# Two accumulating transfers become VectorE additions, and a list scheduler is given ranks

## The chip, the core and the metric

The kernel runs on one core of a Trainium2 chip. TensorE multiplies matrices (at most 128x128 weights against 128x512 data here) into eight banks of PSUM; VectorE, ScalarE and GpSimd work element by element; transfers are started from queues of SyncE (SP), ScalarE and GpSimd and run on 16 DMA engines that these queues share. The metric is the device time of one execution in microseconds.

## The reference

Three layers follow each other, in fp32, for a batch of 2 and a sequence of 768: retention attention with 8 heads of 64, a gated network (`moe`), and a gated network that mixes along the sequence (`moe2`). Cut to what matters:

```python
state = gamma * state + einsum('bhd,bhe->bhde', k[:, :, t], v[:, :, t])   # attention, over t
y[:, :, t] = scale * einsum('bhd,bhde->bhe', q[:, :, t], state)

xk = mu_k * x + (1 - mu_k) * x_prev                  # moe
k = np.maximum(xk @ w_k, 0.0)                        # w_k: 512 x 1024
v = k * k @ w_v                                      # w_v: 1024 x 512
x = v / (1 + exp(-(xr @ w_r)))

h = gelu(x @ w_in); u, v = halves of h               # moe2
v_s = einsum('ts,bsd->btd', w_sg, normalised v) + b_sg
out = x + (u * v_s) @ w_out
```

## The kernel before, in words

Every fp32 product is made of three products of halves: each operand is split into a high part (rounded) and a low part (the rest), and high x high, high x low and low x high are summed in PSUM. `dense` (L326) issues them as three groups. A split is a cast, on ScalarE or VectorE, whichever comes first, and a subtraction on VectorE.

The sequence is done in three blocks of 256 positions (both batches, so 512 columns). Block 0 takes `w_k` and `w_v` directly (`k_tile`, `v_tile`). Blocks 1 and 2 together are done by a Strassen-Winograd scheme with seven products instead of eight: `k_first`, `k_second`, `k_n6`, `k_n5`, `k_m3`, `k_n7`, `k_m4` for `w_k`, and the `v_` functions for `w_v`. The scheme needs sums of quarters of the weights. Those of `w_k` are built in two buffers of the pool `raw`, `k1` and `k3` (128 x 1024): `k_sum_new` starts one on VectorE, `k_sum_dve` (L631) adds one quarter's half on VectorE, and `k_sum_add` (L626) adds one by a transfer from GpSimd's queue that accumulates into `raw`. `k1` goes through three stages that build on each other: after the adds of `aB` half 1 it is split into `s1`, after those of `aA` half 0 into `s2`, and after those of `aA` half 1 into `s4`; `k3` is split into `s3`. The split (`k_split`, L636) writes over quarters of `w_k` that are no longer read. `aA` and `aB` are the two halves of the columns of `w_k`, each with a high and a low tile. In the same way the sums of `w_v` are built by `sum_weights` (L753): an SP transfer starts a sum and GpSimd transfers (L762) accumulate into it.

What sets the order of all this is the class `Plan`. The program is written down as a list of operations, each with an engine, a reckoned cost and its dependences. `order` plays them through: whenever an engine is free, it takes the first operation in the list that is ready and for which there is a buffer. "ADD" stands for GpSimd's queue of accumulating transfers; before, one was reckoned as landing like an ordinary transfer of its size. The order that results is fixed for each engine: an engine runs its instructions one after the other, and one that waits keeps back all behind it.

TensorE's stages, by the names of their outputs in PSUM: `kp` (products with `w_k`), `rp` (with `w_r`), `vp` (with `w_v`, and again with the `v` half of `w_in`), `up` (the `u` half), `sp` (mixing with `w_sg`), `op` (with `w_out`).

Of the kernel before, what the change touches and what calls it, by code (L numbers as in the profile page):

```python
# [47 lines left out]
SLACK = {"raw": 2.0}  # L48
BEGIN = 0.75
ISSUE = 0.4  # L50
ADD_ISSUE = 1.2
DMA_LEAD = 1.4
DMA_TAIL = 2.0
DMA_RATE = 0.41
# [6 lines left out]
class Plan:  # L61


    def __init__(self, slots, quota, most):
        self.ops, self.writer, self.readers, self.users, self.origin = [], {}, {}, {}, {}
        self.slots, self.quota, self.most = slots, quota, most

    def op(self, eng, cost, fn, r=(), w=(), new=(), after=()):
        n = len(self.ops)
        deps = set(after)  # L70
        for k in r:
            deps.update(self.writer.get(k, ()))
        for k in w:
            deps.update(self.writer.get(k, ()))
            deps.update(self.readers.get(k, ()))
        for k in (*r, *w):
            if k[0] in self.origin:
                deps.add(self.origin[k[0]])
        for _, _, buf, _ in new:
            self.origin[buf] = n  # L80
        for k in w:
            self.writer[k], self.readers[k] = [n], []
        for k in r:
            if k not in w:
                self.readers.setdefault(k, []).append(n)
        for k in (*r, *w):
            self.users.setdefault(k[0], set()).add(n)
        self.ops.append((eng, cost, fn, deps, new))

    def order(self):  # L90
        ops, n = self.ops, len(self.ops)
# [19 lines left out]
        link2 = 0.0  # L111
        started = [False] * n

        def put(i):
# [26 lines left out]
            return True  # L141

        def start(i, t, eng):
            nonlocal link, link2
            engs, cost, fn, deps, new = ops[i]
            engs = engs.split()
            if len(engs) > 1:
                cost = cost[engs.index(eng)]
            for e in engs:
                queue[e].remove(i)  # L150
            on[i] = eng
            started[i] = True
# [26 lines left out]
        while events:  # L179
            t = events[0][0]  # L180
            while events and events[0][0] <= t + 1e-9:
                _, i, eng = heapq.heappop(events)
                if eng in SLACK:
                    free[eng] += 1
                elif 0 <= i < n:
                    for k in after[i]:
                        if (ops[k][0] == on[i]) == (eng == "near"):
                            left[k] -= 1
                            if not left[k]:
                                put(k)  # L190
# [21 lines left out]
def fused_kernel(ctx, tc, qk, kv, w_k, w_v, w_r, w_in, w_sg, w_out, consts, ydec, b_sg, out):  # L212
# [11 lines left out]
    T = {}  # L224
# [43 lines left out]
    def convert(name, j, src, dst, tag, part, first):  # L268
# [34 lines left out]
        plan.op("DVE", .69, join, r=[(raw, 1)], w=[(xb, 0)])  # L303
# [430 lines left out]
    def both(out, one, two, op, new=(), sign=None):  # L734
        def go():
            if sign is None:
                dve.tensor_tensor(out=T[out], in0=T[one], in1=T[two], op=op)
            else:
                dve.scalar_tensor_tensor(out=T[out], in0=T[one], scalar=sign, in1=T[two], op0=ALU.mult, op1=op)
        plan.op("DVE", 1.23 if sign is None else 1.32, go, r=[(b, i) for b in (one, two) for i in range(2)], w=[(out, i) for i in range(2)], new=new)  # L740

    def combine(at, one, two, op, first=()):
        (buf, part, view), (ba, pa, va), (bb, pb, vb) = at, one, two
# [140 lines left out]
    for j in range(8):  # L884
        conv("wk", w_k, j, ("aA", "aB"))
    for j in range(8):
        k_tile(0, j)
# [4 lines left out]
    k_first(0)  # L892
    for j in range(1, MK):
        k_first(j)
        k_second(j - 1)
    k_second(MK - 1)
    for m in range(KD):
        prep(0, m, 1)
        conv("wr", w_r, m, ("cA",))
# [1 line left out]
        r_tile(0, m)  # L901
    for m in range(KD):
        for j in range(2):
            conv("wv", w_v, 2 * m + j, ("bA", "bB"))
# [3 lines left out]
    k_sum_dve("k3", "aA", 0, 1)  # L908
    k_sum_add("k1", "aB", 1, 0)
    k_sum_add("k1", "aB", 1, 1)  # L910
    for m in range(KD):
        prep(1, m, 1)
    for m in range(KD):
        r_tile(1, m)
    for m in range(KD):
        prep(2, m, 0, term(2, m), False)
    k_terms()
    for m in range(MK):
        pair_relu(("kf", 1, m // 2), m, 1.0)
# [9 lines left out]
    k_operands("t1", 1, 0)  # L929
    k_n5()  # L930
    for m in range(KD):
        prep(2, m, 1)
    k_split("k3", "s3", "aA", 0, "s2")
    k_split("k1", "s4", "aA", 1)
    k_operands("b22", 2, 1)
    for m in range(MK):
        k_m3(m)
    k_operands("t3", 2, 0)
    k_operands("t4", 1, 1)
    k_n7(0)  # L940
    k_n7(1)
    k_m4(0)
    k_m4(1)
    v_terms(0)
    k_n7(2)
    k_n7(3)
    k_m4(2)
    k_m4(3)
    v_terms(1)
    for m in range(KD):  # L950
        r_tile(2, m)
    v_sums()
    v_direct(1)
    v_weights()
    v_n6()
    v_n5()
    v_sums2()
    v_sums3()
    v_n7()
    for m in range(KD):  # L960
        prep2(0, m)
        conv("win", w_in, m, ("aB", "aA"))
    v_m3()
    v_m4()
    for m in range(KD):
        conv("win", w_in, KD + m, ("aB", "aA"))
        prep2(1, m)
    for m in range(KD):
        prep2(2, m)

# [252 lines left out]
            gating(1, 0, m, half(v), (v, 0), -1)  # L1223

    for j in range(4):
        conv("wout", w_out, j, ("cA",))
    for n in range(NB):
        for b in range(B):
            c1(n, b)
        for m in range(KD):  # L1230
            c2(n, m)
        if n == 0:
            sg("g11", [(0, 0)], "bA", 0)
            sg("g12", [(0, 1)], "bA", 1)
        if n == 1:
            sg("g2", [(0, 0), (1, 0), (1, 1)], "bB", 0)
# [4 lines left out]
    sg_sum("g3", [(0, 0), (1, 0)])  # L1241
    for n in range(NB):
        g_terms(n)
    g_second()
    g_n6()
    g_n5()
    sg_sum("g4", [(0, 0), (0, 1), (1, 0), (1, 1)])
    sg_split("g3", "bA", 0)
# [93 lines left out]
```

## Time and profile before

| | us |
|---|---|
| median of 3 runs | 364.12 (363.67 to 364.89) |
| the profiled execution | 365.24 |
| its span, first to last instruction | 363.5 |
| TensorE busy in the span | 342.7 |
| VectorE, ScalarE, GpSimd busy | 281.2, 194.5, 45.7 |

The profiled execution is 1.12 us above the median. A span is cut by the last instruction; 1.74 us of the execution lie outside it. "Busy" counts the time in which an engine has an instruction at work. A releaser is what ended the idle time of an engine by the profile; where the releaser had itself been waiting, one looks further up its own queue.

### The profile page before, as it was taken

The numbers are of one execution on the slowest core, as the hardware profiler recorded it, in microseconds if no ns is written. First come the engines' busy times: TensorE is split into PE (matmuls) and PEld (weight loads), VectorE is DVE, ScalarE is ACT, GpSimd is POOL, SyncE is SP. The second block draws the span as 40 slices with busy tenths as digits, with TensorE's granted clock in tenths as the row PEclk, the third lists the DMA queues.
The fourth block names the chain that finished last, engine by engine and source line by source line (L and its number), as shares of the span: only waits on it lengthen the run. The fifth ranks groups of instructions, "written<-read, shape, count | busy, mean of one in ns | idle before, by whom it ended". The sixth has DMA issues, their size and how long they took to land.

```text
span 363.5 us, 5464 instructions
## 1 busy us (share of the span) xinstructions
PE 342.7 (94%) x2121; PEld 292.8 (81%) x2121; DVE 281.2 (77%) x479; ACT 194.5 (54%) x306; POOL 45.7 (13%) x42
## 2 busy tenths in 40 slices
PE   8998999999999358699999999999999999999996
PEld 4886888888888246587887888888888999999995
DVE  2599999899976362758989999954658999999832
ACT  1068889799953160656979968822222563514000
POOL 0454400000133222141000000122110000000000
PEclk9999999999999959699999999999999999999999
DMA  8999951136277979396323533899840000000422
GB/s 303 411 409 405 367 175 61 60 115 231 94 119 118 169 152 160 125 176 105 86 89 115 175 115 115 262 207 224 199 65 0 2 2 0 2 0 2 172 88 87
DMA packets 23145, 52.36 MB, mean 144 GB/s; under 512 B 1744, under 2 KB 12368, under 8 KB 23120
## 3 DMA queue, kind: packets, MB, share of 16 engines
q1 hardware_dynamic: 14144, 38.45, 29.4%
q0 software_dynamic: 8688, 12.52, 21.4%
q10 hardware_dynamic: 288, 1.05, 0.7%
q8 instruction: 16, 0.26, 0.3%
q14 instruction: 9, 0.07, 0.1%
HBM read 38.38 MB, written 3.15 MB: 114 GB/s over the span
## 4 chain that ended last, share of the span: by engine, by line
PE 71%; DMA 18%; DVE 4%; issue 3%; ACT 1%; POOL 1%; SPq 0%; DVEq 0%; POOLq 0%; ACTq 0%
PE vp L334 19%; PE kp L334 15%; PE sp L334 11%; PE op L334 9%; PE up L334 9%; PE rp L334 6%; DMA chunk<-kv 6%; DMA raw<-wv 5%; DMA raw<-wk 4%; DMA chunk<-qk 2%; DMA raw<-raw 1%; DVE cv L297 1%; PE y L506 1%; DVE prs L442 1%; DVE raw L623 1%
## 5 line engine op out<-in xcount | busy, mean ns | idle before, releaser
L334 PE MATMUL kp<-xo,wk 128*128 128x512 f32 x264 | 63.8, 401 | 4.3 <-ACT ku L680 4.3
L334 PEld LDWEIGHTS kp<-xo,wk 128*128 128x128 f32 x264 | 50.7, 194 | 16.3 <-ACT ku L680 4.7
L334 PE MATMUL vp<-k,wv 128*128 128x512 f32 x168 | 41.2, 405 | 9.4 <-ACT k L256 9.4
L334 PEld LDWEIGHTS vp<-k,wv 128*128 128x128 f32 x168 | 33.1, 198 | 16.9 <-ACT k L256 9.8
L334 PE MATMUL sp<-sg,vh 128*128 128x384 f32 x252 | 44.6, 335 | 0.1
L334 PEld LDWEIGHTS sp<-sg,vh 128*128 128x128 f32 x252 | 43.7, 188 | 0.8 <-ACT vh L256 0.7
L334 PE MATMUL op<-gt,wout 128*128 128x384 f32 x192 | 33.6, 334 | 0.0
L334 PEld LDWEIGHTS op<-gt,wout 128*128 128x128 f32 x192 | 33.3, 188 | 0.0
L334 PE MATMUL rp<-xo,wr 128*128 128x512 f32 x144 | 33.3, 389 | 0.0
L334 PE MATMUL vp<-win,x2o 128*128 128x512 f32 x144 | 33.3, 389 | 0.0
L334 PE MATMUL up<-x2o,win 128*128 128x512 f32 x144 | 33.1, 389 | 0.0
L334 PEld LDWEIGHTS rp<-xo,wr 128*128 128x128 f32 x144 | 27.0, 188 | 5.6
L334 PEld LDWEIGHTS vp<-win,x2o 128*128 128x128 f32 x144 | 27.0, 188 | 5.6
L334 PEld LDWEIGHTS up<-x2o,win 128*128 128x128 f32 x144 | 27.0, 188 | 5.6
L334 PE MATMUL vp<-k,ws 128*128 128x512 f32 x96 | 22.4, 391 | 0.4 <-DVE k L357 0.4
L282 ACT ACTIVATE cv<-raw 128x512 f32<-128x512 f32 x32 | 21.1, 673 | 3.0 <-DMA raw<-w_out 2.2
L334 PEld LDWEIGHTS vp<-k,ws 128*128 128x128 f32 x96 | 17.9, 188 | 4.6 <-DVE k L357 0.8
L643 DVE TENSOR_TENSOR wk<-raw,wk 128x1024 fp32r<-128x1024 f32 x4 | 4.9, 1226 | 20.8 <-ACT wk L640 20.7
L297 DVE SCALAR_TENSOR_TENSOR cv<-cv,raw 128x512 int32<-128x512 int32 x29 | 20.2, 714 | 0.2 <-ACT raw L290 0.2
L1049 POOL DMA_DIRECT2D raw<-w_sg x7 | 8.4, 1201 | 91.2 <-DVE yy L1002 69.7
L290 ACT ACTIVATE raw<-raw 128x512 int32<-128x512 uint32 x29 | 19.4, 674 | 0.0
L1142 DVE TENSOR_TENSOR o<-op,x 128x256 f32<-128x256 f32 (+1 forms) x32 | 9.7, 352 | 11.6 <-PE op L334 11.5
(144 smaller groups left out, 552.2 us busy)
## 6 DMA issues: line engine op xcount, KB each, us to landing
chunk<-qk SPq DMA_DIRECT2D x12, 512.0 KB, 10.2
chunk<-kv SPq DMA_DIRECT2D x10, 512.0 KB, 10.2
raw<-wv POOLq DMA_DIRECT2D x10, 512.0 KB, 5.5
raw<-w_k SPq DMA_DIRECT2D x8, 512.0 KB, 9.4
raw<-w_v SPq DMA_DIRECT2D x8, 512.0 KB, 3.5
raw<-w_in SPq DMA_DIRECT2D x8, 512.0 KB, 3.4
raw<-w_sg SPq DMA_DIRECT2D x7, 576.0 KB, 5.4
raw<-w_sg POOLq DMA_DIRECT2D x7, 576.0 KB, 6.8
```

Of the source, the lines that this page charges most:

```text
L282: plan.op("ACT", .68, lambda: act.activation(out=xf(), in_=word(1).bitcast(F32), func=ACTF.Prelu, scale=-F64_REBIAS * F64_SIGN, alpha=1.0 ...
L290: act.activation(out=word(0), in_=word(0).bitcast(U32), func=ACTF.Copy, scale=F64_LOW_SCALE, bias=F64_LOW_BIAS)
L297: dve.scalar_tensor_tensor(out=xi(), in0=xi(), scalar=3, in1=word(0), op0=ALU.logical_shift_left, op1=ALU.bitwise_or)
L334: pe.matmul(out=T[ps][:, cols], lhsT=l(), rhs=r(), start=first and q == 0 and i == 0, stop=q == 2 and i == len(grp) - 1, skip_group_check= ...
L442: plan.op("DVE", .66, lambda p=p: dve.tensor_tensor(out=T["pr", i % 4][:, p], in0=heads(T["sc", i, p]), in1=T["mask"].unsqueeze(1).to_broa ...
L506: pe.matmul(out=y_at(i, j, p), lhsT=T["vs", i][:, 2 * j + p], rhs=T["pr", i % 4][:, p, j], start=c == 0 and b == 0 and j < 2, stop=b == B ...
L623: plan.op("DVE", 1.23, lambda: dve.tensor_tensor(out=T[raw], in0=view()[0], in1=view()[1], op=ALU.add), r=keys, w=[(raw, 0)], new=[new("ra ...
L643: plan.op("DVE", 1.23, lambda: dve.tensor_tensor(out=region(tag, half, 1), in0=T[raw], in1=region(tag, half, 0), op=ALU.subtract), r=[(raw ...
L1049: plan.op("ADD", .59, lambda view=view: pool.dma_start(out=T[raw], in_=view, accum_op=ALU.add), w=[(raw, 0)])
L1142: dve.tensor_tensor(out=T[o][:, part], in0=T[ps][:, part], in1=T["x2", n][:, m, of], op=ALU.add),
```

## The change

Two lines that added `aA` half 0 to `k1` by transfers now call `k_sum_dve`. Of the six accumulating transfers of `w_k` four stay. Every step can be given a lead: it is then ranked so many places earlier (or, negative, later) in the scheduler's list, and the scheduler takes the ready operation of lowest rank. 40 or so steps in all stages get one, from -130 to 130. An accumulating transfer is now reckoned to land 5.9 us after its issue, and 3.3 us after the one before it at the earliest, and to hold the queue for 1.3 instead of 1.2 us; two costs of VectorE steps are corrected by 0.03 and 0.09 us. `k_sum_copy` is new, and nothing calls it.

```diff
-ADD_ISSUE = 1.2
+ADD_ISSUE = 1.3
+ADD_TIME = 5.9
+ADD_NEXT = 3.3
@@ Plan.__init__, Plan.op
+        self.lead, self.rank = 0, []
...
+        self.rank.append(n - self.lead)
@@ Plan.order
-                if eng == "AQ":
+                if eng == "ADD":
+                    link3 = done = max(t + ADD_TIME, link3 + ADD_NEXT)
+                elif eng == "AQ":
...
-                for i in sorted(queue[eng], key=lambda i: (eng == "DVE" and ops[i][0] == "DVE ACT", i)):
+                for i in sorted(queue[eng], key=lambda i: (eng == "DVE" and ops[i][0] == "DVE ACT", self.rank[i])):
@@ fused_kernel
+    def led(lead, steps, *args, **more):
+        plan.lead = lead
+        steps(*args, **more)
+        plan.lead = 0
...
-    k_split("k1", "s1", "aB", 0)
-    k_sum_add("k1", "aA", 0, 0)
-    k_sum_add("k1", "aA", 0, 1)
+    led(60, k_split, "k1", "s1", "aB", 0)
+    led(20, k_sum_dve, "k1", "aA", 0, 0)
+    led(90, k_sum_dve, "k1", "aA", 0, 1)
     k_split("k1", "s2", "aA", 0)
...
-    k_split("k3", "s3", "aA", 0, "s2")
-    k_split("k1", "s4", "aA", 1)
+    led(40, k_split, "k3", "s3", "aA", 0, "s2")
+    led(20, k_split, "k1", "s4", "aA", 1)
```

How the instructions move, at three places. Line numbers of the changed kernel are up to 16 higher (L628 is L644 there, L640 is L656, L762 is L778), and buffer numbers differ.

GpSimd's queue of accumulating transfers. Before, from the first transfer of `w_k` on (`wk_738`, `wk_739` are the high and low tile of `aB`, `wk_531`, `wk_532` those of `aA`; the `wv` are the quarters of `w_v`):

```order
L628 DMA raw<-wk_738 128x4x256
L628 DMA raw<-wk_739 128x4x256
L762 DMA raw<-wv_1156 128x2x512
L762 DMA raw<-wv_1157 128x2x512
L628 DMA raw<-wk_531 128x4x256
L762 DMA raw<-wv_1157 128x2x512
L628 DMA raw<-wk_532 128x4x256
L762 DMA raw<-wv_1058 128x2x512
L628 DMA raw<-wk_531 128x4x256
L762 DMA raw<-wv_1059 128x2x512
L628 DMA raw<-wk_532 128x4x256
```

In the changed kernel, from the same transfer on:

```order
L644 DMA raw<-wk_737 128x4x256
L644 DMA raw<-wk_738 128x4x256
L778 DMA raw<-wv_1146 128x2x512
L778 DMA raw<-wv_1147 128x2x512 x2
L644 DMA raw<-wk_531 128x4x256
L644 DMA raw<-wk_532 128x4x256
L778 DMA raw<-wv_1058 128x2x512
L778 DMA raw<-wv_1059 128x2x512
```

The pair of `aA` half 0 is gone. The pair that is left for `aA` (half 1) stands directly one after the other, behind three `wv` transfers instead of between them.

VectorE around the split of `s1`. Before (`raw_1188` is `k1`; `x2` is the gating by `rp` of block 0, `f` the operands of block 2, `k2` the operands of the first product with `w_v`):

```order
L643 TENSOR_TENSOR wk1_739<-raw_1188,wk0_738 128x4x256
L555 SCALAR_TENSOR_TENSOR mix_1263<-x_658,con_110,mix_1263 128x512
L555 SCALAR_TENSOR_TENSOR mix_1275<-x_658,con_110,mix_1275 128x512
L721 TENSOR_TENSOR x2_1071<-vp_1265,x2_1071 128x512
L256 CAST k2_1310<-kf_956 128x1024
L555 SCALAR_TENSOR_TENSOR f_1307<-x_658,con_110,f_1307 128x512 x2
L739 SCALAR_TENSOR_TENSOR f_1331<-f_549,f_1307 128x1024
L737 TENSOR_TENSOR f_1205<-f_1307,f_1205 128x1024
L739 SCALAR_TENSOR_TENSOR f_581<-f_1331,f_581 128x1024
L357 TENSOR_TENSOR k2_1358<-kf_956,k2_1310 128x1024
L643 TENSOR_TENSOR wk1_532<-raw_1188,wk0_531 128x4x256
```

In the changed kernel (`raw_1166` is `k1`):

```order
L656 CAST wk0_737<-raw_1166 128x4x256
L659 TENSOR_TENSOR wk1_738<-raw_1166,wk0_737 128x4x256
L737 TENSOR_TENSOR x2_1055<-vp_1256,x2_1055 128x512
L566 SCALAR_TENSOR_TENSOR f_1303<-x_658,con_110,f_1303 128x512 x2
L649 TENSOR_TENSOR raw_1166<-raw_1166,wk0_531 128x1024
L649 TENSOR_TENSOR raw_1166<-raw_1166,wk1_532 128x1024
L363 TENSOR_TENSOR k2_1343<-kf_922,k2_1305 128x1024
L755 SCALAR_TENSOR_TENSOR f_1351<-f_549,f_1303 128x1024
L363 TENSOR_TENSOR k2_1365<-kf_984,k2_1345 128x1024
L659 TENSOR_TENSOR wk1_532<-raw_1166,wk0_531 128x4x256
L363 TENSOR_TENSOR xo_1378<-f_1351,xo_1367 128x1024
```

The cast of `s1` has moved from ScalarE to VectorE. The two additions stand soon behind it, and the subtraction of `s2` (`wk1_532`) follows five rows after them; the steps on `mix` that stood here have moved.

ScalarE around the casts of the later sums. Before (the first row is the cast of `s2`, the tenth that of `s4`; `vt` and `ku` are copies out of PSUM):

```order
L640 CAST wk0_531<-raw_1188 128x4x256
L256 CAST k2_1360<-kf_1008 128x1024
L715 ACTIVATE x2_1329<-rp_1346 128x512
L715 ACTIVATE x2_1329<-rp_1368 128x512
L256 CAST xo_1394<-f_549 128x1024
L256 CAST xo_1406<-mix_1263 128x512
L256 CAST xo_1409<-mix_1275 128x512
L799 COPY vt_1417<-vp_1387 128x512
L548 ACTIVATE mix_1424<-x_658,omu_131 128x512
L640 CAST wk0_531<-raw_1188 128x4x256
L799 COPY vt_1443<-vp_1411 128x512
L680 COPY ku_1448<-kp_905 128x512
```

In the changed kernel, later in its queue (`raw_1193` is `k3`, its cast that of `s3`; `raw_1166` is `k1`, its cast that of `s4`; `kn` are the copies out of PSUM after n5):

```order
L696 COPY ku_1440<-kp_889 128x512
L696 COPY ku_1450<-kp_904 128x512
L262 CAST xo_1455<-mix_1434 128x512
L696 COPY ku_1464<-kp_932 128x512
L656 CAST wk0_531<-raw_1193 128x4x256
L696 COPY ku_1480<-kp_955 128x512
L656 CAST wk0_531<-raw_1166 128x4x256
L696 COPY kn_1492<-kp_889 128x512
L696 COPY kn_1496<-kp_904 128x512
L696 COPY kn_1505<-kp_932 128x512
L696 COPY kn_1518<-kp_955 128x512
```

The cast of `s4` has moved behind the `ku` copies and stands ahead of the `kn` copies; the cast of `s3`, which VectorE did before, stands on ScalarE between two `ku` copies.

## Rows read from the trace of the kernel before

**Rows 1.** The page, section 1: engine busy us (share of the span) x instructions.
```profile
PE 342.7 (94%) x2121; PEld 292.8 (81%) x2121; DVE 281.2 (77%) x479; ACT 194.5 (54%) x306; POOL 45.7 (13%) x42
```

**Rows 2.** The list of TensorE's waits, 94 us to the end: total, times, longest us.
```profile
PE vp L334 <- ACT k L256: 9.4, 1, 9.4
PE kp L334 <- ACT ku L680: 4.3, 1, 4.3
PE vp L334 <- DVE k L357: 0.4, 1, 0.4
```

**Rows 3.** TensorE's timeline, 110 to 170 us: start, length, instructions [idle before <- releaser].
```profile
110.14 11.04 PE L334 MATMUL rp<-xo,wr 128*128 128x512 f32 x48
121.02 0.61 PE L334 MATMUL vp<-k,wv 128*128 128x512 f32 x2
131.06 7.49 PE L334 MATMUL vp<-k,wv 128*128 128x512 f32 x22 [9.43 <-ACT k L256]
...
148.27 21.75 PE L334 MATMUL kp<-xo,wk 128*128 128x512 f32 x84 [4.29 <-ACT ku L680]
```

**Rows 4.** TensorE by windows: window, us, busy (x instructions), granted clock, DMA share, GB/s.
```profile
121.60:131.06 9.46, 0.04 (x2) 0.71 0.92 176
131.06:138.38 7.32, 7.32 (x22) 0.68 0.90 139
...
148.27:153.00 4.73, 4.73 (x11) 0.51 0.39 152
...
191.70:282.10 90.40, 90.39 (x399) 1.00 0.58 149
```

**Rows 5.** ScalarE's timeline, 110 to 147 us, casts of the sums.
```profile
110.69 1.05 ACT L640 CAST wk<-raw 128x1024 fp32r<-128x1024 f32 x1 [5.93 <-DMA raw<-wk]
...
129.02 1.04 ACT L640 CAST wk<-raw 128x1024 fp32r<-128x1024 f32 x1 [9.33 <-DMA raw<-wk]
...
146.20 1.04 ACT L640 CAST wk<-raw 128x1024 fp32r<-128x1024 f32 x1 [9.27 <-DMA raw<-wk]
```

**Rows 6.** GpSimd's timeline, 98 to 146 us; lengths are of the issue.
```profile
98.82 1.46 POOL L628 DMA_DIRECT2D raw<-wk  x1 [54.97 <-DVE cv L297]
105.10 1.29 POOL L628 DMA_DIRECT2D raw<-wk  x1 [4.82 <-DMA raw<-wk]
...
114.94 2.03 POOL L628 DMA_DIRECT2D raw<-wk  x1
119.91 1.19 POOL L762 DMA_DIRECT2D raw<-wv  x1 [2.94 <-DMA raw<-wv]
...
131.70 1.64 POOL L628 DMA_DIRECT2D raw<-wk  x1
...
139.59 1.32 POOL L628 DMA_DIRECT2D raw<-wk  x1 [2.09 <-DMA raw<-wk]
```

**Rows 7.** VectorE's timeline, 94 to 151 us.
```profile
96.96 1.22 DVE L623 TENSOR_TENSOR raw<-raw,wk 128x1024 f32<-128x1024 f32 x1
...
112.91 1.41 DVE L555 SCALAR_TENSOR_TENSOR mix<-x,con,mix 128x512 f32<-128x512 f32 x2
...
131.23 1.22 DVE L357 TENSOR_TENSOR k<-kf,k 128x1024 fp32r<-128x1024 f32 x1
...
147.28 1.23 DVE L643 TENSOR_TENSOR wk<-raw,wk 128x1024 fp32r<-128x1024 f32 x1 [7.83 <-ACT wk L640]
...
149.38 0.69 DVE L640 CAST wk<-raw 128x1024 fp32r<-128x1024 f32 x1
```

**Rows 8.** Line 628, issue of a `wk` transfer to its landing.
```profile
DMA to landing us min/median/max: 5.6/6.3/7.8
```

**Rows 9.** All engines by windows: busy us of PE, PEld, DVE, ACT, POOL, then clock.
```profile
47.50:94.00 46.50, 46.50 (x205) 38.50 (x206) 42.63 (x68) 41.90 (x74) 0.00 (x0) 1.00 0.41 136
94.00:148.30 54.30, 40.59 (x169) 32.74 (x168) 31.65 (x39) 22.89 (x34) 14.20 (x11) 0.88 0.74 126
94.00:191.70 97.70, 83.62 (x346) 67.53 (x345) 67.03 (x80) 53.98 (x75) 20.37 (x16) 0.91 0.65 124
```

More of the change, by code (lines that the diff above doesn't have):

```diff
@@ L110, in order @@
         seq, events, link = [], [(BEGIN, -1, e) for e in engines], 0.0
-        link2 = 0.0
+        link2 = link3 = 0.0
         started = [False] * n
@@ L143, in start @@
         def start(i, t, eng):
-            nonlocal link, link2
+            nonlocal link, link2, link3
             engs, cost, fn, deps, new = ops[i]
@@ L302, in convert @@
         plan.op("DVE ACT", (.42, .68), lower, r=[(raw, 0)], w=[(raw, 1), (xb, 0)])
-        plan.op("DVE", .69, join, r=[(raw, 1)], w=[(xb, 0)])
+        plan.op("DVE", .72, join, r=[(raw, 1)], w=[(xb, 0)])
         cast(lambda: dst(T[wb][0]), lambda: T[xb], [(xb, 0)], [(wb, ("hi", part))], [first] if first else [])
@@ L624, in k_sum_new, with k_sum_copy @@
                 w=[(raw, 0)], new=[new("raw", "raw", raw, (128, 4, 256))])
+    def k_sum_copy(name, tag, half, h):
+        raw = ("raw", name)
+        plan.op("SP", .53, lambda: sp.dma_start(out=T[raw], in_=wide(tag, half, h)), r=piece_keys(tag, "lo" if h else "hi"),
+                w=[(raw, 0)], new=[new("raw", "raw", raw, (128, 4, 256))])
     def k_sum_add(name, tag, half, h):
@@ L739, in go @@
                 dve.scalar_tensor_tensor(out=T[out], in0=T[one], scalar=sign, in1=T[two], op0=ALU.mult, op1=op)
-        plan.op("DVE", 1.23 if sign is None else 1.32, go, r=[(b, i) for b in (one, two) for i in range(2)], w=[(out, i) for i in range(2)], new=new)
+        plan.op("DVE", 1.23, go, r=[(b, i) for b in (one, two) for i in range(2)], w=[(out, i) for i in range(2)], new=new)
     def combine(at, one, two, op, first=()):
@@ L886, in fused_kernel @@
     for j in range(8):
-        k_tile(0, j)
+        led(-110, k_tile, 0, j)
     for i in range(2):
@@ L891, in fused_kernel @@
         k_operands(("b11", "b21")[i], 1, i)
-    k_first(0)
+    led(40, k_first, 0)
     for j in range(1, MK):
         k_first(j)
-        k_second(j - 1)
-    k_second(MK - 1)
+        led(70, k_second, j - 1)
+    led(-80, k_second, MK - 1)
     for m in range(KD):
@@ L903, in fused_kernel @@
         for j in range(2):
-            conv("wv", w_v, 2 * m + j, ("bA", "bB"))
+            led(-20, conv, "wv", w_v, 2 * m + j, ("bA", "bB"))
         v_tile(0, m)
@@ L907, in fused_kernel @@
     k_sum_new("k3", lambda: (T["raw", "k1"], wide("aA", 0, 0)), [(("raw", "k1"), 0), *piece_keys("aA", "hi")])
-    k_sum_dve("k3", "aA", 0, 1)
+    led(10, k_sum_dve, "k3", "aA", 0, 1)
     k_sum_add("k1", "aB", 1, 0)
-    k_sum_add("k1", "aB", 1, 1)
+    led(-20, k_sum_add, "k1", "aB", 1, 1)
     for m in range(KD):
-        prep(1, m, 1)
+        led(-40, prep, 1, m, 1)
     for m in range(KD):
@@ L915, in fused_kernel @@
     for m in range(KD):
-        prep(2, m, 0, term(2, m), False)
-    k_terms()
+        led(20, prep, 2, m, 0, term(2, m), False)
+    led(-30, k_terms)
     for m in range(MK):
-        pair_relu(("kf", 1, m // 2), m, 1.0)
+        led(-80, pair_relu, ("kf", 1, m // 2), m, 1.0)
     v_direct(0)
-    k_split("k1", "s1", "aB", 0)
-    k_sum_add("k1", "aA", 0, 0)
-    k_sum_add("k1", "aA", 0, 1)
+    led(60, k_split, "k1", "s1", "aB", 0)
+    led(20, k_sum_dve, "k1", "aA", 0, 0)
+    led(90, k_sum_dve, "k1", "aA", 0, 1)
     k_split("k1", "s2", "aA", 0)
@@ L931, in fused_kernel @@
     for m in range(KD):
-        prep(2, m, 1)
-    k_split("k3", "s3", "aA", 0, "s2")
-    k_split("k1", "s4", "aA", 1)
-    k_operands("b22", 2, 1)
+        led(30, prep, 2, m, 1)
+    led(40, k_split, "k3", "s3", "aA", 0, "s2")
+    led(20, k_split, "k1", "s4", "aA", 1)
+    led(-100, k_operands, "b22", 2, 1)
     for m in range(MK):
@@ L938, in fused_kernel @@
     k_operands("t3", 2, 0)
-    k_operands("t4", 1, 1)
-    k_n7(0)
+    led(-20, k_operands, "t4", 1, 1)
+    led(10, k_n7, 0)
     k_n7(1)
@@ L943, in fused_kernel @@
     k_m4(1)
-    v_terms(0)
+    led(-90, v_terms, 0)
     k_n7(2)
     k_n7(3)
-    k_m4(2)
+    led(20, k_m4, 2)
     k_m4(3)
@@ L952, in fused_kernel @@
     v_sums()
-    v_direct(1)
+    led(-20, v_direct, 1)
     v_weights()
@@ L956, in fused_kernel @@
     v_n5()
-    v_sums2()
+    led(80, v_sums2)
     v_sums3()
-    v_n7()
+    led(130, v_n7)
     for m in range(KD):
-        prep2(0, m)
-        conv("win", w_in, m, ("aB", "aA"))
+        led(-40, prep2, 0, m)
+        led(60, conv, "win", w_in, m, ("aB", "aA"))
     v_m3()
@@ L966, in fused_kernel @@
         conv("win", w_in, KD + m, ("aB", "aA"))
-        prep2(1, m)
+        led(30, prep2, 1, m)
     for m in range(KD):
@@ L1225, in fused_kernel @@
     for j in range(4):
-        conv("wout", w_out, j, ("cA",))
+        led(-30, conv, "wout", w_out, j, ("cA",))
     for n in range(NB):
@@ L1232, in fused_kernel @@
         if n == 0:
-            sg("g11", [(0, 0)], "bA", 0)
+            led(-40, sg, "g11", [(0, 0)], "bA", 0)
             sg("g12", [(0, 1)], "bA", 1)
         if n == 1:
-            sg("g2", [(0, 0), (1, 0), (1, 1)], "bB", 0)
+            led(20, sg, "g2", [(0, 0), (1, 0), (1, 1)], "bB", 0)
             sg("g1", [(1, 0), (1, 1)], "bB", 1)
@@ L1240, in fused_kernel @@
     g_first()
-    sg_sum("g3", [(0, 0), (1, 0)])
+    led(120, sg_sum, "g3", [(0, 0), (1, 0)])
     for n in range(NB):
-        g_terms(n)
+        led(-130, g_terms, n)
     g_second()
[L1245 to L1248, printed above, removed]
+    led(-40, g_n6)
+    led(-50, g_n5)
+    led(40, sg_sum, "g4", [(0, 0), (0, 1), (1, 0), (1, 1)])
+    led(80, sg_split, "g3", "bA", 0)
     sg_split("g4", "bA", 1)
-    sg("g22", [(1, 1)], "bB", 0)
-    g_n7()
-    g_m3()
+    led(-40, sg, "g22", [(1, 1)], "bB", 0)
+    led(30, g_n7)
+    led(10, g_m3)
     g_m4()
@@ L1256, in fused_kernel @@
         gt_split(1, 1, m, half(("gw", m)), (("gw", m), 0))
-    c4(0, 1)
+    led(10, c4, 0, 1)
     c4(1, 1)
@@ L1260, in fused_kernel @@
         gt_split(1, 0, m, half(("gv", m)), (("gv", m), 0))
-    c4(1, 0)
+    led(20, c4, 1, 0)
     last = {}
```

## The prediction, made before the changed kernel was run

> **What bounds the kernel now.** I read the page first: TensorE is busy for 342.7 of 363.5 us [rows 1], so it is the bound, and what a change can win is the time in which TensorE stands still or runs at a lower clock. The list of TensorE's waits shows where it stands still: 9.4 us before a `vp` product, 4.3 us before a `kp` product, 0.4 us before another `vp`, and nothing more from 94 us to the end [rows 2]. The timeline of TensorE puts the first two at 121.63 to 131.06 us and 143.98 to 148.27 us [rows 3]. Cutting the windows there shows the second price: the granted clock is 0.71 in the first gap, 0.68 in the 7.32 us after it, and 0.51 in the 4.73 us after the second, that is, part or nearly all of such a stretch at 1.2 instead of 2.4 GHz. From 191.7 to 282.1 us it is 1.00 with no gap [rows 4].
>
> The releaser named in both waits is ScalarE (`k` L256, `ku` L680), but ScalarE's timeline shows that it only stood in a queue: at 129.02 us it starts a `wk` cast of L640 (1.04 us) after 9.33 us of idling for a transfer, and the `k` cast that TensorE wants stands between its end at 130.06 and TensorE's start at 131.06; at 146.20 us the same with 9.27 us, and the `ku` copy stands behind it [rows 5]. Those transfers are the accumulating ones. GpSimd's timeline has six of `wk` interleaved with those of `wv` [rows 6]. So the cause is a chain of transfers, and the engine named is only its messenger.
>
> **What the change removes.** The additions of `aA` half 0 to `k1` leave GpSimd's queue and become VectorE additions of 128x1024. The order shows six `wk` transfers before and four after, so two go, not four. I price them by VectorE's first sums of the same shape, 1.22 us each [rows 7]. Before, the pair runs from 114.94 us until the cast at 129.02 us: 14.1 us [rows 5, 6]. Now it is two steps of 1.22 us.
>
> What goes from TensorE's path:
> 1. the first gap, 9.43 us [rows 3];
> 2. the low clock behind it: 22 products took 7.32 us [rows 4]; at the 0.2267 us of each `rp` product (48 of them from 110.14 to 121.02 us [rows 3]) they take 4.99, so 2.33 us;
> 3. the second gap, 4.29 us [rows 3], if the last `wk` transfer now lands in time (below);
> 4. the low clock behind that: 11 products in 4.73 us [rows 4] against 2.49, so 2.24 us.
>
> Sum: 18.29 us. The 0.4 us gap may move, so I don't count it.
>
> **Is the last sum in time now?** This is the step everything hangs on. `s4`, the sum from `aA` half 1, still takes two accumulating transfers, and its cast still stands in ScalarE's queue ahead of the `kn` copies. When TensorE wants it: `rp` ends at 121.02 us, then come 24 products of `v_direct(0)`, 24 of n6 and 24 of n5, 72 x 0.2267 = 16.3, so `m3` asks at 137.3 us. When it comes, with the early part as before: `s1` is complete at 110.69 us (the first two transfers, from 98.82 us, unchanged [rows 5, 6]); on VectorE its cast (0.69) and subtraction (1.2) give 112.6; then the order has one gate and two `f` steps (about 2.0), the two new additions (2.3), two `k` subtractions and an `f` step of 1.1 to 1.2 each, and the subtraction of `s2` (1.2), whose cast ScalarE has done by then: 121.5 us [rows 7]. The next transfer is issued some 0.6 us later, as at 98.82 us after the VectorE sum that ended at 98.18 [rows 6, 7]. Its pair before took from 131.70 to 146.15 us, 14.45 us [rows 5, 6], which gives 136.5, and the cast of 1.05 us ends at 137.6. That is 0.3 us late. The other end: the new order puts the `k3` sum ahead of a `cv` step and a `wv` subtraction of 0.6 us each, and I expect it 1.9 us earlier, which gives 135.7, in time. Transfers vary: the six took 5.6 to 7.8 us [rows 8]; all four at 7.8 instead of 11.87 and 14.45 us for the pairs make it 4.9 us later. So this step costs between 0 and 5.2 us; I take 0.2, next to the nearest pair.
>
> GpSimd runs in order, and the first of that pair now stands behind three `wv` transfers. The third of these was issued at 119.91 us [rows 6], with 1.19 us of issue: GpSimd is free at 121.1, before 122.1. TensorE wants the `wv` sums only after 216 more products (24 + 120 `kp` + 48 `rp` + 24), at some 170 us, so their own delay by a transfer or two stays hidden.
>
> **What the two additions cost.** 2.4 us on VectorE, in a stretch, 94 to 148.3 us, where it is busy for 31.65 of 54.30 us [rows 9]: hidden. With no such cover they would cost at most their 2.4 us.
>
> **The ranks.** They move instructions on every engine. TensorE's products keep their number and sort, so the cost can only be new waits. From 47.5 to 94 us VectorE is busy for 42.63 us and ScalarE for 41.90 of 46.50 us, while TensorE has no gap [rows 9]; orders that tight already run without loss, which bounds the cost from one side at 0. From the other, from 94 to 191.7 us VectorE has 67.03 us of work [rows 9], with the new additions 69.5, and the stretch shrinks from 97.7 to 79.4 us: 88% busy, with 9.9 us to spare. If a third of that spare is needed at the wrong places it costs 3.3 us. I take 1.3, nearer to the dense stretch that had no gap. The one swap on SP, a `kv` load ahead of a `w_k` load, moves each by one issue; I cost it at 0.
>
> **Sum.** The profiled execution took 365.24 us, 363.5 of it the span. 365.24 - 18.29 + 0.2 + 1.3 = 348.45 us. The median of the runs shown, 364.12, lies 1.12 lower, so the prediction is 347.3 us.
>
> Do VectorE's instructions hold up GpSimd's transfers? The first `wk` transfer, with VectorE at work beside it, took at most 6.28 us (98.82 to 105.10); the last, at most 6.61 (139.59 to 146.20), ran while VectorE idled for 7.83 us [rows 5 to 7]. So nothing here says they do. A rule of the Trainium skill speaks against more work on VectorE: the page "SBUF — State Buffer", section "Who interferes with whom", says that VectorE copies and casts in a two-port mode lock GpSimd out of writing the descriptors of its transfers, while an addition of two tensors takes only the read side. By it the new additions lengthen nothing, in agreement with these rows; the casts that the new order puts on VectorE might, which is the third rival.
>
> **Rivals.**
> - *The first gap goes, the second stays, smaller.* The transfers of `s4` fall at the slow end: 4.9 us later, a gap of 5.2 us, and 2.24 us of low clock behind it as after the 4.29 us gap. For it: the margin is near zero and TensorE's queue has nothing else to do there. Against: half of the slow end would have to happen in each of four transfers. 365.24 - 18.29 + 1.3 + 5.2 + 2.24 - 1.12 = 354.6 us.
> - *VectorE and ScalarE become the bound between 121 and 190 us.* The work that used to fall into the gaps has to be done beside TensorE's. For it: 88% on VectorE. Against: 92% from 47.5 to 94 us with no gap [rows 9]. At the 3.3 us above, and as much again in the last stage whose order is changed too: 365.24 - 18.29 + 0.2 + 6.6 - 1.12 = 352.6 us.
> - *Slower: longer transfers stop all engines in order.* The place is the cast of `s1`, which now stands on VectorE, and the cast of `s4` on ScalarE: everything behind them waits. With a transfer of a us, `s4` is ready at 98.8 + 2a + 11.4 + 2a + 1.05 us, and the loss against 137.3 is 4a - 26.1. It eats the gain (18.29 less 2.24 for the clock) from a = 10.5 us on. At a = 12: 365.24 - 18.29 + 21.9 + 2.24 + 1.3 - 1.12 = 371.3 us. For it: VectorE is busier beside the transfers than now. Against: 7.8 us is the longest of six [rows 8], and those beside a busy VectorE are no longer.
> - *The change doesn't do what it says* holds in part: two transfers, not four. It changes nothing above, since the sum is made from the order as it stands.
>
> **How the numbers follow.** Forecast 0.66, its own range 344 to 351 (no new loss at all, 345.8, less the 0.4 us gap, the noise and what other small gaps may give; above, both middle losses doubled and the noise). First rival 0.13, second 0.14, third 0.04; 0.03 for something unseen. The range of 344 to 354 us holds the forecast, the second rival and half of the first. About 0.3% (1.1 us) is what a measurement of this kernel can tell from no change. Faster by more than that: everything but the third rival and the unseen, 0.93. Within 0.3%: 0.02; slower: 0.05.
>
> **What would show it.** Right: four `wk` transfers on GpSimd; TensorE with no gap over 1 us from 121 to 165 us and a granted clock of 1.00 there; the last `wk` cast on ScalarE ends before or near 137.5 us; TensorE starts the gating products (`sp`) near 265 us instead of 282 (where the dense window ends [rows 4]). Wrong: a gap before the `kp` products of `m3` with the transfer as ScalarE's wait (first rival); many waits of 0.3 to 1 us on VectorE or ScalarE (second); transfers of `wk` over 8 us (third); a TensorE gap before 94 us, where I count none.

## The result and the profile after

| | before | changed | ratio (95%) |
|---|---|---|---|
| median, us | 364.5 (4 runs, 363.67 to 365.12) | 344.65 (4 runs, 344.53 to 344.85) | 0.9457 (0.9435 to 0.9479) |
| the profiled execution, us | 365.24 | 344.56 | |
| its span, us | 363.5 | 342.8 | |

The change saves 19.85 us. The forecast was 347.3, with a range of 344 to 354: the right way and inside the range, but 2.65 us too long.

The page of the changed kernel, section 1, against [rows 1]: TensorE's busy time has fallen by 6.0 us, with the same 2121 products.

```profile
PE 336.7 (98%) x2121; PEld 290.5 (85%) x2121; DVE 282.4 (82%) x482; ACT 194.3 (57%) x305; POOL 42.8 (12%) x40
```

The list of TensorE's waits for the whole span, without one of 0.2 us, against [rows 2]:

```profile
PE warm L417 <- DVE x L526: 1.2, 1, 1.2
PE sc L444 <- DMA chunk<-qk: 1.2, 1, 1.2
```

The reader is to see what is missing: the waits of 9.4, 4.3 and 0.4 us are gone, and the longest left is 1.2 us, before 47 us. TensorE's timeline, against [rows 3] (start, length, instructions):

```profile
47.03 30.22 PE L340 MATMUL kp<-xo,wk 128*128 128x512 f32 x132
...
109.73 11.04 PE L340 MATMUL rp<-xo,wr 128*128 128x512 f32 x48
120.61 5.60 PE L340 MATMUL vp<-k,wv 128*128 128x512 f32 x24
126.05 24.64 PE L340 MATMUL kp<-xo,wk 128*128 128x512 f32 x108
...
262.05 39.19 PE L340 MATMUL sp<-sg,vh 128*128 128x384 f32 x225
```

No row has an idle time in brackets. The 24 products of `v_direct(0)` run through, and the 108 of n6, n5, m3 and what follows them start where they end. The products with `w_sg` (`sp`) start at 262.05 us instead of 282.09. All engines by windows, against [rows 9] (busy us of PE, PEld, DVE, ACT, POOL, then granted clock, DMA share, GB/s):

```profile
94.00:148.30 54.30, 54.30 (x242) 44.97 (x241) 47.62 (x59) 34.05 (x49) 13.49 (x12) 1.00 0.71 136
94.00:180.00 86.00, 86.00 (x382) 71.22 (x380) 77.34 (x94) 60.51 (x84) 17.25 (x14) 1.00 0.69 141
```

TensorE fills both windows, at a granted clock of 1.00; VectorE is busy for 77.34 of 86 us, 90%, and TensorE doesn't wait for it. GpSimd's timeline, against [rows 6]:

```profile
96.68 1.45 POOL L644 DMA_DIRECT2D raw<-wk  x1 [54.06 <-ACT kf L684]
104.01 1.29 POOL L644 DMA_DIRECT2D raw<-wk  x1 [5.88 <-DMA raw<-wk]
...
120.78 1.31 POOL L644 DMA_DIRECT2D raw<-wk  x1 [0.71 <-DVE wk L659]
127.55 1.28 POOL L644 DMA_DIRECT2D raw<-wk  x1 [5.46 <-DMA raw<-wk]
```

Four `wk` transfers, the last two one after the other. ScalarE's timeline, against [rows 5]: the cast of `s4`.

```profile
133.76 1.05 ACT L656 CAST wk<-raw 128x1024 fp32r<-128x1024 f32 x1 [0.98 <-DMA raw<-wk]
```

The cast of `s4` starts at 133.76 us, after 0.98 us of idling instead of 9.27, and ends at 134.81. `m3` asks for it when n6 and n5 are through: 126.05 + 48 x 0.2267 = 136.9 us. VectorE's timeline, against [rows 7]: the last cast of an `rp` operand (`xo` from `mix`), the cast of `s1`, the two new additions (2.48 us for both) and the subtraction of `s2`, which ends at 120.4 us.

```profile
106.48 0.48 DVE L262 CAST xo<-mix 128x512 fp32r<-128x512 f32 x1
...
109.60 0.69 DVE L656 CAST wk<-raw 128x1024 fp32r<-128x1024 f32 x1 [1.24 <-DMA raw<-wk]
...
113.39 2.48 DVE L649 TENSOR_TENSOR raw<-raw,wk 128x1024 f32<-128x1024 f32 x2
...
119.19 1.22 DVE L659 TENSOR_TENSOR wk<-raw,wk 128x1024 fp32r<-128x1024 f32 x1
```

Issue to landing of the `wk` transfers, against [rows 8]:

```profile
DMA to landing us min/median/max: 5.6/6.3/7.0
```

### The profile page after: what moved, and what is told of

Its sections match the earlier page's. It is cut to its first block, busy times and chain, and to the rows that moved or that the text cites. A ratio compares the mean times of both kernels' runs of the same rounds, so it can differ in the third digit from the quotient of the medians.

```text
span 342.8 us, 5447 instructions
## 1 busy us (share of the span) xinstructions
PE 336.7 (98%) x2121; PEld 290.5 (85%) x2121; DVE 282.4 (82%) x482; ACT 194.3 (57%) x305; POOL 42.8 (12%) x40
## 4 chain that ended last, share of the span: by engine, by line
PE 93%; DVE 5%; issue 0%; DVEq 0%
PE vp L340 27%; PE kp L340 17%; PE sp L340 13%; PE op L340 10%; PE up L340 10%; PE rp L340 10%; PE sc L444 3%; PE y L517 2%; PE warm L417 2%; DVE prs L453 1%; DVE mix L566 1%; PE y L506 1%; DVE cv L303 1%; DVE x L531 1%; PE st L480 1%; DVE xo L329 1%
## 5 line engine op out<-in xcount | busy, mean ns | idle before, releaser
L340 PE MATMUL kp<-xo,wk 128*128 128x512 f32 x264 | 61.0, 391 | 0.0
L340 PEld LDWEIGHTS kp<-xo,wk 128*128 128x128 f32 x264 | 49.3, 188 | 10.6 <-issue 0.3
L340 PE MATMUL vp<-k,wv 128*128 128x512 f32 x168 | 39.1, 389 | 0.0
L340 PEld LDWEIGHTS vp<-k,wv 128*128 128x128 f32 x168 | 31.5, 188 | 6.5
L303 DVE SCALAR_TENSOR_TENSOR cv<-cv,raw 128x512 int32<-128x512 int32 x28 | 19.7, 717 | 0.2
L296 ACT ACTIVATE raw<-raw 128x512 int32<-128x512 uint32 x28 | 18.7, 672 | 0.0
L453 DVE TENSOR_TENSOR prs<-sc,con 128x512 f32<-128x512 f32 x24 | 15.2, 683 | 2.8 <-PE sc L444 2.7
## 6 DMA issues: line engine op xcount, KB each, us to landing
chunk<-qk SPq DMA_DIRECT2D x12, 512.0 KB, 10.1
```

The lines of the kernel that those rows point to most:

```text
L296: act.activation(out=word(0), in_=word(0).bitcast(U32), func=ACTF.Copy, scale=F64_LOW_SCALE, bias=F64_LOW_BIAS)
L303: dve.scalar_tensor_tensor(out=xi(), in0=xi(), scalar=3, in1=word(0), op0=ALU.logical_shift_left, op1=ALU.bitwise_or)
L340: pe.matmul(out=T[ps][:, cols], lhsT=l(), rhs=r(), start=first and q == 0 and i == 0, stop=q == 2 and i == len(grp) - 1, skip_group_check= ...
L453: plan.op("DVE", .66, lambda p=p: dve.tensor_tensor(out=T["pr", i % 4][:, p], in0=heads(T["sc", i, p]), in1=T["mask"].unsqueeze(1).to_broa ...
```

## The experiments

Twelve kernels, each timed in three rounds; the ratios are to the kernel before in the same rounds, whose medians were 364.17 to 364.38 us. In the short diffs `+` is against the kernel named ahead of them. "The swap" is the two VectorE additions, "the leads" the ranks, "the reckoning" the new costs.

**1. The swap alone**, against before:

```diff
-    k_sum_add("k1", "aA", 0, 0)
-    k_sum_add("k1", "aA", 0, 1)
+    k_sum_dve("k1", "aA", 0, 0)
+    k_sum_dve("k1", "aA", 0, 1)
```

> The kernel before with the two VectorE additions alone: no leads, the old reckoning. Theory 1 (the chain of wk transfers was what TensorE waited for, so the swap does nearly all of the gain): the gap before v_direct(0) is gone; the pair for s4 now stands behind four wv transfers and has a fifth between its two, so its cast ends at 137 to 141 us against some 137 when TensorE asks: a gap of 0 to 4 us and 0 to 2.2 us of low clock, so 345.5 to 351 us. Theory 2 (without the ranks the other engines don't follow, and the swap alone gives half or less): 354 us or more, with waits of VectorE or ScalarE steps spread over 121 to 190 us.

Measured 360.74 us, 0.9899 (0.9873 to 0.9926). Theory 1, on which the prediction was built, falls: the swap by itself is worth some 3.5 us. Theory 2's time holds, but not its picture: there are no waits spread over 121 to 190 us. TensorE's two long waits from 47 us on, GpSimd's timeline, and VectorE's around the cast of `s4` in this kernel:

```profile
PE kp L334 <- DVE wk L640: 5.3, 1, 5.3
PE kp L334 <- DVE xo L357: 4.1, 1, 4.1
```

```profile
128.10 1.33 POOL L762 DMA_DIRECT2D raw<-wv  x1 [7.46 <-DMA raw<-raw]
128.82 1.93 POOL L628 DMA_DIRECT2D raw<-wk  x1
133.70 1.18 POOL L762 DMA_DIRECT2D raw<-wv  x1 [2.96 <-DMA raw<-wv]
136.90 1.29 POOL L628 DMA_DIRECT2D raw<-wk  x1 [2.02 <-DMA raw<-wk]
```

```profile
122.89 1.22 DVE L643 TENSOR_TENSOR wk<-raw,wk 128x1024 fp32r<-128x1024 f32 x1
...
142.77 0.69 DVE L640 CAST wk<-raw 128x1024 fp32r<-128x1024 f32 x1 [12.14 <-DMA raw<-wk]
```

The first gap is down to 0.55 us, but where the second was there are now two, of 5.3 and 4.1 us. The subtraction of `s2` ends at 124.1 us, but the `wk` transfer that waits for it goes out at 128.82: ahead of it in GpSimd's queue a `wv` transfer waited 7.46 us, until 128.10, for the copy from which its sum starts (`raw<-raw`). A second `wv` transfer splits the pair. VectorE then stands 12.14 us at the cast, with other steps behind it. So theory 3 took the place of theory 1, to be tested in runs 7, 9 and 11: TensorE waits for steps that stand, in the fixed order of GpSimd and of VectorE or ScalarE, behind a step that waits for a transfer. What would count is that order.

**2. The swap undone**, against the changed kernel (`led(20, k_sum_add, ...)` and `led(90, k_sum_add, ...)` in place of the two `k_sum_dve`).

> The changed kernel with its two new VectorE additions turned back into accumulating transfers; leads and reckoning stay. Theory 1: six wk transfers again, s2 some 11 us later than in the changed kernel and s4 as much, two TensorE gaps again, with 2.2 us of low clock behind each: 355 to 364 us. Theory 2 (the ranks, which move the k cast out from behind the cast of s2, do most of it): 346 to 351 us.

Measured 351.84 us, 0.9651 (0.9623 to 0.9679): below theory 1's 355, 0.84 above theory 2's end. Six transfers with the new order lose 7.2 us, not 19.85. TensorE's waits:

```profile
PE kp L340 <- DVE wk L656: 3.0, 1, 3.0
PE vp L340 <- ACT k L262: 1.7, 1, 1.7
```

**3. The leads at nought**, against the changed kernel (`self.rank.append(n)`).

> The changed kernel with all leads at nought; swap and reckoning stay. Theory 1: 345 to 349 us, as the swap with the old reckoning or less. Theory 2: 352 us or more.

Measured 348.27 us, 0.9564 (0.9537 to 0.9591), as theory 1 had it, so the leads are worth 3.6 us here. TensorE's longest wait (the other is 0.4 us):

```profile
PE kp L340 <- DVE wk L656: 1.1, 1, 1.1
```

**4. The old reckoning**, against the changed kernel (the diff of `Plan.order`, `ADD_ISSUE` and the two VectorE costs reversed).

> The changed kernel with the old reckoning of accumulating transfers and of the two VectorE steps; swap and leads stay. Theory 1: 344.5 to 349 us; if a gap comes back it is the one before m3, since three wv transfers stand ahead of the s4 pair and one stands inside it. Theory 2 (the leads are fitted to the reckoning and are worthless without it): 350 us or more.

Measured 357.93 us, 0.9833 (0.9802 to 0.9864). The time is theory 2's: 13.3 us are lost by a few reckoned costs. But the leads are not worthless without the reckoning: this kernel is still 2.8 us faster than run 1, which has the swap alone. TensorE's waits:

```profile
PE kp L338 <- ACT ku L694: 5.1, 1, 5.1
PE rp L338 <- DVE xo L327: 2.9, 1, 2.9
```

**5 and 6. The leads alone, and the reckoning alone** (the swap and the other part undone in the changed kernel).

> The kernel before with the leads alone: six wk transfers, the old reckoning. After the swap alone took 360.7 us, and the changed kernel with the old reckoning 357.9, theory 3 says that the three parts only work together, because what counts is where the wk transfers stand in GpSimd's queue, and with the old reckoning a wv transfer goes between them: 360 to 366 us, both gaps there. Theory 4 (the parts add up: the swap 7.2, the reckoning 13.3, the leads 3.6 us as each costs when taken out) says 359.5 to 361.5 us.

> The kernel before with the new reckoning alone: six wk transfers, no leads. Theory 3: the scheduler now puts the last wk pair back to back, but six transfers one after the other are still too long: a gap before m3, 352 to 358 us. Theory 4: 364.2 less 13.3, so 350 to 352 us.

Measured 362.78 us, 0.9949 (0.993 to 0.9969), and 356.36 us, 0.9773 (0.975 to 0.9797): theory 3 both times. TensorE's waits with the leads alone, then with the reckoning alone:

```profile
PE kp L338 <- ACT ku L694: 10.5, 1, 10.5
PE vp L338 <- ACT x L729: 3.5, 1, 3.5
```

```profile
PE kp L340 <- DVE wk L656: 6.9, 1, 6.9
```

All eight combinations are now there, in us (before: 364.2 to 364.5):

| | neither | leads | reckoning | both |
|---|---|---|---|---|
| transfers | 364.3 | 362.78 | 356.36 | 351.84 |
| the swap | 360.74 | 357.93 | 348.27 | 344.65 |

Each alone gives 3.6, 1.5 and 7.9 us, 13.0 together; the whole change gives 19.7. The parts don't add up, and the reckoning is the largest, whatever it is added to.

**7. GpSimd's queue alone.** Against run 1, whose order the other engines keep:

```diff
 k_sum_add("k1", "aA", 1, 1)
+late.append(len(plan.ops) - 1)
...
             r=[...], w=keep,
+            after=late if name == "s2" else ()
```

> The kernel before with the swap, old reckoning and no leads, as the one that took 360.7 us, and one thing more: the two wv transfers of the sum s2 may not be issued before the last wk transfer. On the other engines the order is the same. Theory 3 (a wv transfer that waits 7.5 us for the copy its sum starts from holds up the wk pair behind it in GpSimd's queue, and a second one splits the pair): the pair goes out at some 124.7 instead of 128.8 us, and lands by 138; the 5.3 us gap shrinks to 1 us or less, the 4.1 us one behind it, where VectorE's own order holds TensorE, stays for the most part: 353 to 357 us. Rival (the transfers are slow by themselves, or the data come late): 359.5 us or more.

Measured 354.81 us, 0.9727 (0.9692 to 0.9761): 5.9 us less than run 1, as theory 3 said. GpSimd's timeline, VectorE's, and the row of TensorE behind its longest gap (two of 1.06 and 0.38 us are left elsewhere):

```profile
124.95 1.31 POOL L628 DMA_DIRECT2D raw<-wk  x1 [3.79 <-DVE wk L643]
132.10 1.28 POOL L628 DMA_DIRECT2D raw<-wk  x1 [5.84 <-DMA raw<-wk]
```

```profile
137.73 0.69 DVE L640 CAST wk<-raw 128x1024 fp32r<-128x1024 f32 x1 [6.62 <-DMA raw<-wk]
...
142.61 1.22 DVE L357 TENSOR_TENSOR xo<-f,xo 128x1024 fp32r<-128x1024 f32 x1
```

```profile
143.89 15.84 PE L334 MATMUL kp<-xo,wk 128*128 128x512 f32 x58 [4.61 <-DVE xo L357]
```

The pair goes out at 124.95 us, and the cast starts at 137.73 instead of 142.77. The `xo` subtraction that TensorE waits for stands behind it, with other steps of the sums between.

**8. Two more additions on VectorE**, against the changed kernel (`k_sum_dve` for `aA` half 1 too).

> The changed kernel with the additions of aA half 1 to k1 on VectorE too: two wk transfers left. If TensorE is the bound from 47 us to the end in the changed kernel, as its trace shows, nothing is left to win there: 344 to 345.2 us. Rival (VectorE, with 2.4 us more in a stretch where it is 90% busy from 94 to 180 us, gets late): 346 to 349 us.

Measured 344.91 us, 0.9459 (0.9441 to 0.9478): no difference from the changed kernel. TensorE is the bound there.

**9. VectorE's order alone.** Against run 7:

```diff
-    k_split("k1", "s4", "aA", 1)
     k_operands("b22", 2, 1)
+    first.append(len(plan.ops) - 1)
+    k_split("k1", "s4", "aA", 1)
@@ k_split, the cast
-     after=users(old[0]))
+     after=users(old[0]) | set(first))
```

> The kernel of the last study that holds the two wv transfers back (354.8 us), and one thing more: VectorE's cast of s4 stands behind the subtraction of the operand b22 instead of five steps ahead of it. All else is in the same order. Theory 3 (VectorE, in order, waits 6.6 us at that cast for the wk transfer, and the operand that TensorE wants stands behind it): the gap of 4.6 us shrinks to 1 us or less and the low clock behind it goes: 347.5 to 350 us. Rival (the operand is late for another reason, such as its own data): 353 us or more.

Measured 347.76 us, 0.9533 (0.9506 to 0.956): moving the cast of `s4`, and with it its own subtraction, behind other steps on one engine is worth 7.05 us. VectorE's timeline and TensorE's row behind the gap:

```profile
134.69 1.22 DVE L357 TENSOR_TENSOR xo<-f,xo 128x1024 fp32r<-128x1024 f32 x1
138.01 0.69 DVE L642 CAST wk<-raw 128x1024 fp32r<-128x1024 f32 x1 [2.10 <-DMA raw<-wk]
```

```profile
138.85 14.24 PE L334 MATMUL kp<-xo,wk 128*128 128x512 f32 x60 [0.24 <-DVE wk L642]
```

The subtraction starts at 134.69 us, before the cast stands waiting, and the 4.61 us gap is 0.24 us. The transfer landed no earlier: the cast starts at 138.01 us, against 137.73 in run 7. This shows the mechanism by itself: the data and the order of the transfers are the same, and only what stands behind the waiting step is another.

**10 and 12. The reckoning in two halves**, against the changed kernel: the old reckoning of the transfers alone (run 10), the two old VectorE costs alone (run 12).

> The changed kernel with the old reckoning of the accumulating transfers alone; the two corrected VectorE costs (0.03 and 0.09 us) stay. Theory 5 (what set the queue's order in the run with the old reckoning, 357.9 us, was not the reckoned length of the transfers but the two small costs): the wk pair stands back to back as in the changed kernel, 344.5 to 346 us. Theory 6 (the reckoned length did it): 354 us or more.

> The changed kernel with the two old VectorE costs (0.03 and 0.09 us off) and the new reckoning of the transfers. Theory 5: a wv transfer goes between the wk pair again, and the time is near that of the run with all of the old reckoning: 350 to 358 us. Theory 6: 344.5 to 347 us.

Measured 354.79 us, 0.9727 (0.9696 to 0.9758), and 344.95 us, 0.9456 (0.9432 to 0.9479). By the times theory 5 falls: the reckoned length of the transfers is worth 10.1 us, and beside it the two small costs are worth 0.3, which is within the noise. With the old length they are not small: runs 4 and 10 differ by them alone, and lie 3.1 us apart. On the queue theory 5 was right: with swap and leads in place, the small costs decide whether the pair stands together (run 10 and the changed kernel) or is split (runs 4 and 12). So the new length does not win its time by the pair standing together. In run 10 the pair does so, and TensorE loses 6.52 us elsewhere, here in TensorE's, VectorE's and ScalarE's timelines:

```profile
118.01 13.22 PE L338 MATMUL rp<-xo,wr 128*128 128x512 f32 x45 [6.52 <-ACT xo L260]
```

```profile
110.45 1.23 DVE L657 TENSOR_TENSOR wk<-raw,wk 128x1024 fp32r<-128x1024 f32 x1 [5.03 <-ACT wk L654]
111.71 2.48 DVE L647 TENSOR_TENSOR raw<-raw,wk 128x1024 f32<-128x1024 f32 x2
...
115.31 0.74 DVE L564 SCALAR_TENSOR_TENSOR mix<-x,con,mix 128x512 f32<-128x512 f32 x1
```

```profile
109.36 1.05 ACT L654 CAST wk<-raw 128x1024 fp32r<-128x1024 f32 x1 [6.21 <-DMA raw<-wk]
...
117.36 0.60 ACT L260 CAST xo<-mix 128x512 fp32r<-128x512 f32 x1
```

With the transfers reckoned too short, the scheduler believes `s1` complete early and places its subtraction and the two new additions ahead of the `xo` and `mix` steps of `rp`. VectorE waits there until 110.45 us for ScalarE's cast, which itself idled for the transfer, so the `mix` step comes at 115.31, its cast at 117.36, and the `rp` product at 118.01. In the changed kernel the last cast of such an operand (106.48) stands ahead of the cast of `s1` (109.60). This is read from the traces; no run moved these steps by themselves. In run 12, on the other hand, a `wv` transfer does split the pair, and nothing is lost; GpSimd's timeline:

```profile
119.76 1.29 POOL L644 DMA_DIRECT2D raw<-wk  x1 [5.41 <-DVE wk L659]
121.79 1.19 POOL L778 DMA_DIRECT2D raw<-wv  x1 [0.74 <-DMA raw<-raw]
125.54 1.29 POOL L644 DMA_DIRECT2D raw<-wk  x1 [2.56 <-DMA raw<-wk]
```

That `wv` transfer waited only 0.74 us, and the cast of `s4` started at 132.78 us, 13.02 after the first issue.

**11. Run 4 with the two `wv` transfers held back**, the edit of run 7.

> The changed kernel with the old reckoning, as the run that took 357.9 us, with the two wv transfers of the sum s2 held back until the wk pair is out. Theory 3: the last wk transfer lands 4 to 5 us earlier, the gap of 5.1 us and the low clock behind it go, that of 2.9 us before an rp product, which VectorE's order makes, stays: 349 to 352 us. Rival (the queue's order matters little there): 356 us or more.

Measured 351.77 us, 0.9644 (0.9615 to 0.9672): theory 3. The 5.1 us gap is gone, and the one of 2.9 before `rp`, made by VectorE's order as in run 10, stays.

No run is faster than the changed kernel; runs 8 and 12 equal it. No other values of the reckoned times were run. So it is shown that these values give a better order than the old ones, but not that they do it by being nearer to the measured times; the 3.1 us between runs 4 and 10 show how far small changes of a cost move the order by themselves.

## Why the prediction was right, and where it was not

**The gaps and the clock, 18.29 us: right.** From the start of the dense `kp` stretch (47.42 us before, 47.03 after) to the first `sp` product the time fell from 234.67 to 215.02 us, by 19.65. The rows of TensorE before that this rests on, and that [rows 3] does not have:

```profile
47.42 30.24 PE L334 MATMUL kp<-xo,wk 128*128 128x512 f32 x132
...
169.87 2.88 PE L334 MATMUL rp<-xo,wr 128*128 128x512 f32 x12
...
282.09 42.45 PE L334 MATMUL sp<-sg,vh 128*128 128x384 f32 x240
```

The 19.65 us hold the 18.29, the third gap of 0.38 us, which was not counted, and some 0.16 us at each of three gaps: the last product before a gap takes 0.39 us to end (0.61 us for two in [rows 3]), where a dense row charges 0.2267 for it. The rest lies in two rows. The 84 products behind the second gap took 21.60 us, from 148.27 to 169.87, where a dense row takes 19.04: 2.56 us more, and not the 2.24 that were counted; nearly all of the difference is lost from 163.90 us on, at two products far behind the low clock. The 70 products behind the third gap took 16.04 us, where a dense row takes 15.87, at a granted clock of 1.00. What these 0.32 and 0.17 us wait for is open.

**`s4` in time, 0.2 us: it cost nothing.** It was put 0.3 us late and came early. The subtraction of `s2` ended at 120.4 us instead of 121.5, the transfer went out at 120.78 instead of 122.1, and the pair took 12.98 us (120.78 to 133.76) instead of the 14.45 taken from [rows 5, 6]. Runs 7 and 12 have pairs as short (12.78 and 13.02 us), the second with a `wv` transfer between. The record shows where pairs are long. Where the first transfer of a pair went out within 0.9 us of a `wv` transfer, the second, which waits for it, followed after 7.8 to 9.1 us (before, runs 1, 5, 10 and 11); in all other pairs that waited for nothing else, after 5.8 to 7.5 us (6.77 in the changed kernel, 1.89 us behind a `wv` transfer). Why is not shown.

**The two additions on VectorE, nothing: right.** Run 8 put two more there, again for nothing.

**The leads, 1.3 us between 0 and 3.3: the step that failed.** The prediction said that, since TensorE's products keep their number and sort, "the cost can only be new waits", and bounded it from one side at 0. No new waits came, and an order that is changed can take waits away as well: without the leads the changed kernel loses 3.6 us (run 3). Part of that are gaps before the first `sp` product (1.07 and 0.38 us in run 3), which the 18.29 already counts as gone. What the leads bring on top of it is 0.7 us in the last stage, which takes 80.66 to 80.76 us from the first `sp` product in each of the eight kernels with leads and 81.36 to 81.42 in the six without. So the term should have been about -0.7 us, not 1.3.

**The sum.** 348.45 us stood against a profiled execution of 344.56. Of the 3.89 us, 1.5 are the two terms above that cost nothing, 0.66 the last stage, 0.39 the stretch before 47 us (it ends at 47.03 to 47.42 us over all fourteen kernels, so this may be scatter), 0.38 the third gap, 0.48 the ends of three rows, 0.32 and 0.17 the rows behind the second and the third gap. The 1.12 us between profile and median did not recur (344.56 against 344.65). It is luck that taking them off brought the forecast nearer, from 3.80 us too long to 2.65.

**The cause.** Here the prediction was right for a reason that it gave only in part. It put the whole 18.29 us under what the two removed transfers free, but the swap alone gives some 3.5 us (run 1) and taking it out costs 7.2 (run 2). Its numbers came out because they were worked from the order of the changed kernel as it stands (the pair behind three `wv` transfers, the cast of `s4` behind the `ku` copies), and that order doesn't come about without the reckoning (run 4 keeps the swap and the leads and loses 13.3 us), to which the prediction gave no term at all. Its sentence that the engine named "is only its messenger" was half right: the chain of transfers sets when the waiting step goes on, but what TensorE loses depends on what stands behind that step. Run 9 won 7.05 us with the transfers where they were.

**The rivals.** None came. The second (VectorE and ScalarE as the bound) is excluded by run 8. The third named the right place, the cast of `s1` on VectorE with everything behind it, but for longer transfers. They were no longer than before (5.6 to 7.0 us with VectorE 88% busy from 94 to 148.3 us, 47.62 of 54.30, against 5.6 to 7.8 with 31.65). The rule of the Trainium skill that the prediction weighed (page "SBUF — State Buffer", section "Who interferes with whom", VectorE's two-port copies and casts shut GpSimd out of writing descriptors) is therefore not seen to cost anything here. But these rows hardly test it: none of VectorE's casts falls into one of the four issues of the changed kernel (the nearest starts at 129.01 us, 0.18 us after the last issue ends), and no run measured it by itself.

## What to carry to other kernels

Where engines run in a fixed order, a step that waits for a transfer costs what stands behind it, on the engine that waits and in the queue that issues: look in the trace at the rows behind a long idle, not only at the transfer that ended it. In a list scheduler, look at the reckoned length of slow transfers before removing them; here the new reckoning alone was worth 7.9 us, and removing two of six alone 3.6. And take such a change apart with each part alone and each part out, since the gain of parts that share one cause does not add up.

## What the runs showed of the hardware that was not expected

Whether the granted clock fell after an idle of TensorE didn't go by the length of that idle alone. Windows right behind a gap: in run 2 behind 3.02 us and behind 1.72 us, then in run 5 behind 3.52 us (window, us, busy, granted clock, DMA share, GB/s):

```profile
143.12:146.00 2.88, 2.88 (x7) 0.50 1.12 193
184.00:187.00 3.00, 2.99 (x13) 1.00 0.82 269
```

```profile
128.87:134.00 5.13, 5.13 (x23) 1.00 0.67 110
```

The level is 1.2 GHz (0.50) behind the 3.02 us gap, and 2.4 GHz (1.00) behind both the shorter one and the longer one of 3.52 us. Why the last kept its clock is open; no run was made for it.
